# Local attention and FFN block: logits and AV sums by column groups, the AV result turned by DMA, softmax with its maximum, LN2 sums on ScalarE, other FFN groups

## The chip, the cores and the metric

The kernel runs on one core of a Trainium2 chip. The metric is the device time of one launch in microseconds (us). The core has TensorE (PE, matrix products; PEld are its weight loads), VectorE (DVE), ScalarE (ACT), GpSimd (POOL) and SyncE (SP, which here issues nearly all DMAs), all running side by side and waiting for each other by semaphores.

## The reference

A transformer block with adaptive layer norm over 2048 tokens of width 512:

```python
mod = silu(c) @ w_mod                       # shifts, scales, gates: sa, ca, ga, sb, cb, gb
h = layernorm(x) * (1 + ca) + sa            # LN1
q, k, v = h @ wqkv                          # 32 heads of 16
idx = pos[:, None] - 2 * arange(8)          # each token sees itself and 7 earlier ones, 2 apart
logits = einsum('bhsd,bhswd->bhsw', q, k[idx]) * 16 ** -0.5, masked where idx < 0
attn = softmax(logits, axis=-1)             # over the 8 places
o = einsum('bhsw,bhswd->bhsd', attn, v[idx])
x = x + ga * (o @ wo)
h = layernorm(x) * (1 + cb) + sb            # LN2
x = x + gb * ((silu(h @ w1) * (h @ w3)) @ w2)   # FFN of width 1792
```

## The kernel before, in words

Tokens are worked in 16 tiles of 128 (T). Activations are bf16, sums are fp32 in PSUM (8 banks of 128x512). `_build` (L351) records operations with their engine, estimated cost and data; `Program.schedule` (L143) then puts them in an order by a table of priorities (L955) and hands out buffers and banks; `synchronize` (L242) derives the semaphore waits. Each engine then runs its own list strictly in order. The arrays FFN (L341), BLOCKS (L342), DMA_T (L345) and LATE (L347) say which tiles form a group, which groups turn their normalized rows by DMA, and when late weight loads are issued.

The stages, by line:
- The start: warm-up products on ones (L551), modulation columns (L535), gates (L565, spread at L575). SP loads x, the modulation weights and wqkv (all DMAs are issued at L135). LN1 groups of 2, 2, 4, 4, 4 tiles: statistics on DVE (`ln_stats`, L590, L591), the power on POOL (L596, L598), normalizing on DVE (L613), turning on PE (L649), scale and shift on ACT (L657).
- Q and K products (L702), copied by ACT (L710, L711); V products (L721), copied (L731) and stored to DRAM, from where V comes back as shifted rows, 4 loads of 256 KB a tile (in `values`).
- Logits of a tile: DVE multiplies Q with the 8 shifted K (L752, 128x4096); PE sums each head's 16 features: 32 products with the multiplied block (128x128) as weights and a 32-column indicator E moving (L761). Tokens are then on partitions.
- Softmax (`exps`, `softmax`): ACT takes exp straight from PSUM (L775) without a maximum; DVE adds in three steps (L791, L793, L795), takes a reciprocal (L797) and scales (L798); tile 0 is masked by a multiply (L787).
- AV (`values`, L803): the weights go to DRAM and come back turned (two DMAs a tile), DVE multiplies the shifted V by them (L821), PE sums over the 8 places with 32 products of 16 columns (L830), which come out with features on partitions; ACT copies (L836); PE multiplies by wo (L843); DVE adds to x (L847).
- LN2: statistics on DVE as in LN1, the bias on DVE (L603), normalizing on ACT (L609), turning on PE for the first three groups (L649) and by DMA for the last two, modulation on ACT (L657, L634).
- FFN in groups of 2, 4, 4, 4, 2 tiles: 14 slices, each of w1 and w3 products (L859, 256 or 512 columns), silu on ACT (L865), product on DVE (L868); then w2 (L897, halves of 256 columns in the last two tiles, L885), the last add (L907) and the store.

## Time and profile before

| what | before |
|---|---|
| median of 3 runs (lowest to highest) | 250.9 us (250.34 to 252.05) |
| profiled execution: span, first to last instruction | 248.6 us |
| profiled execution: own time | not listed apart from the three runs; their median lies 2.3 us over the span |
| ACT busy | 123.3 us |
| DMA packets, bytes | 49393, 37.09 MB |

The page gives each engine's busy time, then 40 slices of the span, DMA queues, the chain of work that ended last (followed back from the last instruction, at each step to what released it), and groups of equal instructions: line, engine, operation, output and inputs, count, then busy us and mean ns of one, then the idle time of its engine just before them. Products are pipelined, so the mean of one (379 ns for 512 columns) is longer than their spacing. SPq is SP's queue, "issue" time in which nothing shown was waited for.

### The profile page before, as it was taken

Reading aid. Unit: us, or ns where it says so; the run is one execution under the profiler, and the core shown is the slowest. Engines: PE = TensorE matmul, PEld = TensorE weight load, DVE = VectorE, ACT = ScalarE, POOL = GpSimd, SP = SyncE. Lnnn points to the kernel's source line nnn. Section 1 sums busy time; section 2 is a strip of 40 time slices with the busy share of each in tenths; the row PEclk is TensorE's granted clock in tenths of the full one; section 3 lists DMA queues with packets and bytes.
Section 4 is the critical chain, followed back from the end, with each engine's and each line's share of the span. In section 5 each row is a group of like instructions: output and inputs, shape, how many; then the busy total and the mean of one; then the engine's idle time right before and its main releaser. Section 6 shows DMA issues by size and latency. Waiting matters only on the chain.

```text
span 248.6 us, 5772 instructions
## 1 busy us (share of the span) xinstructions
PE 243.5 (98%) x2437; PEld 149.2 (60%) x2437; DVE 186.8 (75%) x289; ACT 123.3 (50%) x216; POOL 21.3 (9%) x48
## 2 busy tenths in 40 slices
PE   8989999999999999999999999999999999999995
PEld 8857665475778856545665564455544444465784
DVE  3869799999898999999899897898942344232442
ACT  2369688864783466943230577443556333110320
POOL 3223500003200110000001101000110000000000
PEclk9999999999999999999999999999999999999999
DMA  6999969679979993336779270436032000001001
GB/s 221 356 327 274 279 201 299 140 199 286 314 223 259 319 288 100 63 54 157 200 232 263 56 229 22 85 46 169 3 84 63 4 0 0 21 24 42 21 3 42
DMA packets 49393, 37.09 MB, mean 149 GB/s; under 512 B 22216, under 2 KB 40664, under 8 KB 49368
## 3 DMA queue, kind: packets, MB, share of 16 engines
q1 hardware_dynamic: 49360, 36.73, 53.3%
q8 instruction: 19, 0.31, 0.5%
q14 instruction: 6, 0.05, 0.1%
q10 hardware_dynamic: 8, 0.00, 0.0%
HBM read 30.67 MB, written 5.26 MB: 145 GB/s over the span
## 4 chain that ended last, share of the span: by engine, by line
PE 94%; DMA 4%; SPq 1%; issue 0%; DVE 0%
PE pall L859 39%; PE pall L897 17%; PE pall L702 11%; PE pall L843 6%; PE pall L721 6%; PE pall L761 5%; PE pall L830 5%; DMA sb_wqkv<-in_A_wqkv_dram 4%; PE pall L885 2%; PE pall L649 2%; SPq L135 1%; PE pall L535 0%; PE pall L565 0%; PE pall L575 0%; DVE sb_o L907 0%
## 5 line engine op out<-in xcount | busy, mean ns | idle before, releaser
L859 PE MATMUL pall<-sb_h,sb_w 128*128 128x512 bf16 (+1 forms) x560 | 101.2, 336 | 0.0
L859 PEld LDWEIGHTS pall<-sb_h,sb_w 128*128 128x128 bf16 x560 | 53.8, 98 | 41.4
L865 ACT ACTIVATE sb_sg<-pall 128x512 bf16<-128x512 f32 (+1 forms) x70 | 35.3, 511 | 64.3 <-PE pall L859 64.3
L868 DVE TENSOR_TENSOR sb_hh<-sb_sg,pall 128x512 bf16<-128x512 bf16 (+1 forms) x70 | 39.0, 575 | 28.4 <-PE pall L859 28.4
L897 PE MATMUL pall<-sb_w,sb_hh 128*128 128x512 bf16 x196 | 44.4, 379 | 0.0
L752 DVE TENSOR_TENSOR sb_pq<-sb_q,sb_kT 128x4096 bf16<-128x4096 bf16 x16 | 36.1, 2280 | 0.5 <-ACT sb_kT L711 0.5
L702 PE MATMUL pall<-sb_h,sb_wqkv 128*128 128x512 bf16 (+1 forms) x160 | 31.0, 336 | 1.4 <-DMA sb_wqkv<-in_A_wqkv_dram 1.4
L897 PEld LDWEIGHTS pall<-sb_w,sb_hh 128*128 128x128 bf16 x196 | 18.9, 98 | 21.1
L821 DVE TENSOR_TENSOR sb_vsh<-sb_vsh,sb_al 128x4096 bf16<-128x4096 bf16 x12 | 27.2, 2283 | 0.4 <-DMA sb_al<-a_scratch_dram 0.2
L590 DVE BATCH_NORM_STATS2 sb_st<-sb_x 128x6 f32<-128x512 bf16 x32 | 21.7, 678 | 4.6 <-DMA sb_x<-in_A_x_dram 4.3
L907 DVE TENSOR_TENSOR sb_o<-pall,sb_x 128x512 bf16<-128x512 f32 (+1 forms) x18 | 11.2, 629 | 17.9 <-PE pall L897 13.6
L657 ACT ACTIVATE sb_h<-pall,sb_modc 128x512 bf16<-128x512 bf16 (+1 forms) x30 | 19.2, 706 | 7.8 <-PE pall L649 7.7
L702 PEld LDWEIGHTS pall<-sb_h,sb_wqkv 128*128 128x128 bf16 x160 | 15.0, 98 | 12.9 <-issue 1.6
L596 POOL TENSOR_TENSOR sb_rs<-sb_mv,sb_cst 128x2 f32<-128x2 f32 x16 | 5.2, 326 | 159.0 <-DVE sb_mv L591 159.0
L609 ACT ACTIVATE sb_xn<-sb_x,sb_nb,sb_rs 128x512 bf16<-128x512 bf16 x16 | 12.1, 805 | 11.5 <-DVE sb_nb L603 11.5
L836 ACT ACTIVATE sb_ot<-pall 128x512 bf16<-128x512 f32 x16 | 9.5, 597 | 15.6 <-PE pall L830 13.7
L761 PEld LDWEIGHTS pall<-sb_E,sb_pq 128*128 128x128 bf16 x512 | 14.8, 96 | 2.9
L843 PE MATMUL pall<-sb_wo,sb_ot 128*128 128x512 bf16 x64 | 15.8, 378 | 0.0
L721 PE MATMUL pall<-sb_wqkv,sb_h 128*128 128x512 bf16 x64 | 15.6, 379 | 0.0
L761 PE MATMUL pall<-sb_E,sb_pq 128*128 128x32 bf16 x512 | 15.0, 176 | 0.0
L598 POOL TENSOR_TENSOR sb_rs<-sb_rs,sb_cst 128x2 f32<-128x2 f32 x16 | 13.9, 871 | 1.3
L710 ACT ACTIVATE sb_q<-pall 128x512 bf16<-128x512 f32 (+1 forms) x20 | 10.2, 517 | 6.6 <-PE pall L702 6.5
(69 smaller groups left out, 196.0 us busy)
## 6 DMA issues: line engine op xcount, KB each, us to landing
sb_vsh<-v_scratch_dram SPq DMA_DIRECT2D x48, 256.0 KB, 4.5
sb_vshx<-v_scratch_dram SPq DMA_DIRECT2D x16, 256.0 KB, 5.3
sb_w<-in_B_w_dram SPq DMA_DIRECT2D x6, 512.0 KB, 7.3
sb_w<-in_B_w_dram SPq DMA_DIRECT2D x6, 384.0 KB, 5.7
v_scratch_dram<-sb_v SPq DMA_DIRECT2D x16, 128.0 KB, 5.3
out_dram<-sb_o SPq DMA_DIRECT2D x14, 128.0 KB, 1.8
sb_wqkv<-in_A_wqkv_dram SPq DMA_DIRECT2D x3, 512.0 KB, 10.0
sb_x<-in_A_x_dram SPq DMA_DIRECT2D x3, 512.0 KB, 10.4
```

The source lines that it names most:

```text
L590: o = p.op("dve", lambda e, m=m, T=T: e.bn_stats(st[:, m, :], x_sb[:, T, :]), 670, ("st", m), r=[vx[T]], w=[vs])
L657: return e.activation(vh.at[:, ft, 0:n * P], b[:, j * 512:j * 512 + n * P], ACT.Identity, bias=modc[:, 8 * which + ft:8 * which + ft + 1], ...
L702: ins = e.matmul(bank(vp)[:, 0:n], wqkv[:, t, col:col + P], vh.at[:, t, 0:n], start=(t == ORDER[0]), stop=(t == ORDER[-1]))
L721: ins = e.matmul(bank(vp), vh.at[:, t, tt * P:(tt + 1) * P], wqkv[:, t, 2 * D:3 * D], start=(t == ORDER[0]), stop=(t == ORDER[-1]))
L752: return e.tensor_tensor(vp.at[:], in0, in1, ALU.mult)
L761: ins = e.matmul(b[:, c0:c0 + H], vp.at[:, w, ft, :], E_sb[:, ft, :], start=(ft == 0), stop=(ft == KT - 1))
L821: return e.tensor_tensor(v_w, v_w, a_w, ALU.mult)
L843: ins = e.matmul(bank(vy), vt.at[:, ft, :], wo[:, ft, :], start=(ft == 0), stop=(ft == KT - 1))
L859: ins = e.matmul(bank(vp)[:, 0:n], wt[:, t, fi * P:(fi + 1) * P], vh.at[:, t, 0:n], start=(t == 0), stop=(t == KT - 1))
L865: p.op("act", lambda e: e.activation(vt.at[:, 0:n], bank(vgp)[:, 0:n], ACT.Silu), c_act(n), k, r=[vgp], w=[vt], table="silu")
L868: p.op("dve", lambda e: e.tensor_tensor(vh_.at[:, 0:n], vt.at[:, 0:n], bank(vup)[:, 0:n], ALU.mult), c_dve(n), k, r=[vt, vup], w=[vh_])
L897: ins = e.matmul(bank(vz), vhh[fi].at[:, tt * P:(tt + 1) * P], w2[:, fi, :], start=(fi == 0), stop=(fi == NF - 1))
```

## The change

- Logits: E becomes the weights, 32 columns wide, and the multiplied block moves, 256 columns at a time; four products write the four groups of 32 PSUM partitions by `tile_position`. 16 products a tile instead of 32; heads now lie on partitions, with 32 tokens and 8 places along the row. Tile 0's mask is a first product that adds a large negative number.
- Softmax: DVE takes the maximum over the 8 places from PSUM and writes the differences; ACT takes exp of them in SBUF; DVE sums in one step, takes the reciprocal and scales. All groups are pairs of tiles.
- The weights are turned by PE (two transposes a tile) and copied by ACT; the DRAM buffer for them is gone.
- AV sums: a 32-column indicator is the weights and the multiplied V moves, 512 columns; 8 products a tile in four column groups. The result has tokens on partitions; ACT copies it and a DMA transpose on SP turns it.
- The residual add also sums its row; LN2 makes its mean from that on POOL, and ACT sums squares of the centred row (`Square` with `accum_out`), 16 of them; POOL makes variance, power and bias. DVE has no LN2 statistics any more.
- FFN groups 2, 2, 4, 4, 2, 2; groups from the third on (12 tiles, formerly 6) are turned by DMA.
- The order of all operations and the buffers are now lists in the file (ORDER, SLOTS), and GATES ties late loads to logits or AV multiplies. In the new order SP issues x rows of tiles 2 to 7, the first gate's weights and x of tiles 8 to 11 ahead of the K weights (before: tiles 2 to 7 alone); the first FFN product stands behind the logits of 9 tiles (before: 8 tiles), and all of LN1, Q, K and V; the third FFN group's first w2 product stands behind all 16 logits. Warm-up products are one of 512 columns in place of four of 128. LN1, Q, K, V, wo and the FFN's arithmetic are as before.

The core of the diff:

```diff
-        p.schedule(_priorities())
+        p.place(ORDER, SLOTS)
-FFN = [[0, 1], [2, 3, 4, 5], [6, 7, 8, 9], [10, 11, 12, 13], [14, 15]]
-BLOCKS = [[[0]], [[1]], [[2, 3]], [[4, 5]], [[6, 7]], [[8, 9]], [[10, 11]], [[12, 13], [14, 15]]]
-VG = 2
+FFN = [[0,1],[2,3],[4,5,6,7],[8,9,10,11],[12,13],[14,15]]
+BLOCKS = [[[0, 1]], [[2, 3]], [[4, 5]], [[6, 7]], [[8, 9]], [[10, 11]], [[12, 13], [14, 15]]]
-DMA_T = (5, 3)
+DMA_T = (5, 2)
+GATES = [-1, 6, 8, 3, 2, 2, 14, 12, 10, 0, 16, 18, 12, 14, 12, 7, 13, 13, 8, 3]
...
+    def ln_sums(Ts):
+
+        n, i, k = len(Ts), Ts[0], ("st", NT + Ts[-1])
+        vnm, vvs, vns = Val("nmean"), [], [Val("xn", xnpool) for T in Ts]
+        p.op("pool", lambda e: e.tensor_scalar(nm[:, i:i + n, 0], sx[:, i:i + n, 0], -1.0 / D, None, op0=ALU.mult), 250, k,
+             r=[vsx[T] for T in Ts], w=[vnm])
+        for T, vn in zip(Ts, vns):
+            vv = Val("var")
+            p.op("act", lambda e, vn=vn, T=T: e.activation(vn.at[:], x_sb[:, T, :], ACT.Square, bias=nm[:, T, :],
+                                                    accum_out=var[:, T, :]), c_act(512) + 230, ("st", NT + T), r=[vx[T], vnm],
+                 w=[vv, vn])
+            vvs.append(vv)
+        va, vr, vb = Val("vare"), Val("rstd"), Val("nbias")
+        rsn = rs[:, NT + i:NT + i + n, 0]
+        o = p.op("pool", lambda e: e.tensor_scalar(rsn, var[:, i:i + n, 0], 1.0 / D, EPS, op0=ALU.mult, op1=ALU.add), 300, k, r=vvs, w=[va])
+        o = p.op("pool", lambda e: e.tensor_tensor(rsn, rsn, bass.AP(cst, 1, [[2, P], [0, n]]), ALU.pow), 600, k, r=[va, vcst],
+                 w=[vr], lead=o)
+        p.op("pool", lambda e: e.tensor_tensor(nb[:, i:i + n, 0], nm[:, i:i + n, 0], rsn, ALU.mult), 250, k, r=[vr, vnm], w=[vb], lead=o)
+        for T, vn in zip(Ts, vns):
+            p.op("act", lambda e, vn=vn, T=T: e.activation(vn.at[:], x_sb[:, T, :], ACT.Identity, bias=nb[:, T, :],
+                                                           scale=rs[:, NT + T, :]),
+                 c_act(512) + 230, ("nm", NT + T), r=[vx[T], vr, vb], w=[vn])
         return vns
 
...
-            def red(e, i=i, vp=vp):
-                b = bank(vl)
-                for w in range(W):
-                    for ft in range(KT):
-                        c0 = i * W * H + w * H
-                        ins = e.matmul(b[:, c0:c0 + H], vp.at[:, w, ft, :], E_sb[:, ft, :], start=(ft == 0),
-                                       stop=(ft == KT - 1))
+            def red(e, i=i, T=T, vp=vp):
+                c0 = vl.at * 512 + i * W * 32
+                if T == 0:
+                    e.matmul(PALL[0:32, c0:c0 + W * 32], ones[:, 0:32], before[:], start=True, stop=False, tile_position=(0, 0))
+                for ft in range(KT):
+                    for q in range(4):
+                        ins = e.matmul(PALL[32 * q:32 * q + 32, c0:c0 + W * 32], E_sb[:, ft, :], bass.AP(vp.at, ft * P + 32 * q, [[W * KT * P, P], [KT * P, W], [1, 2], [2, 16]]),
+                                       start=(ft == 0 and (T > 0 or q > 0)), stop=(ft == KT - 1), tile_position=(0, 32 * q))
                 return ins
 
-            p.op("pe", red, C_RED, ("lg", T), r=[vp, vE], part=[vl])
+            p.op("pe", red, C_RED + (110 if T == 0 else 0), ("lg", T), r=[vp, vE] + ([vbefore, vc] if T == 0 else []), part=[vl], tiled=True)
         return vl
-    def exps(groups, vls):
-
-        ves = [Val("ex", smpool) for _ in groups]
-
-        def ex(e):
-            for Ts, vl, ve in zip(groups, vls, ves):
-                n = len(Ts) * W * H
-                ins = e.activation(ve.at[1].rearrange("p t w h -> p (t w h)")[:, 0:n], bank(vl)[:, 0:n], ACT.Exp)
-            return ins
-
-        p.op("act", ex, sum(c_act(len(g) * W * H) for g in groups), ("ex", groups[0][0]), r=vls, w=ves, table="exp")
-        return ves
-
-    def softmax(Ts, ve):
+    def shift(Ts, vl):
 
         n = len(Ts)
         k = ("sm", Ts[0])
-        o = None
-        if Ts[0] == 0:
-            o = p.op("dve", lambda e: e.tensor_tensor(ve.at[1][:, 0], ve.at[1][:, 0],
-                                                      bass.AP(mask0, 0, [[W, P], [1, W], [0, H]]), ALU.mult),
-                     430, k, r=[vmask0], w=[ve], lock=True)
-        vs1, vs2, vs3, vr, va = Val("s1"), Val("s2"), Val("s3"), Val("rsum"), Val("attn")
-        o = p.op("dve", lambda e: e.tensor_tensor(ve.at[2][:, 0:n], ve.at[1][:, 0:n, 0:4], ve.at[1][:, 0:n, 4:8], ALU.add),
-                 75 + 134 * n, k, r=[ve], w=[vs1], lead=o, lock=True)
-        o = p.op("dve", lambda e: e.tensor_tensor(ve.at[2][:, 0:n, 0:2], ve.at[2][:, 0:n, 0:2], ve.at[2][:, 0:n, 2:4], ALU.add),
-                 75 + 67 * n, k, r=[vs1, ve], w=[vs2], lead=o, lock=True)
-        o = p.op("dve", lambda e: e.tensor_tensor(ve.at[3][:, 0:n], ve.at[2][:, 0:n, 0], ve.at[2][:, 0:n, 1], ALU.add),
-                 75 + 34 * n, k, r=[vs2, ve], w=[vs3], lead=o, lock=True)
-        o = p.op("dve", lambda e: e.reciprocal(ve.at[3][:, 0:n], ve.at[3][:, 0:n]), 75 + 267 * n, k, r=[vs3, ve], w=[vr], lead=o, lock=True)
+        ve, vm, vs = Val("ex", smpool), Val("max"), Val("shifted")
+        o = p.op("dve", lambda e: e.tensor_reduce(ve.at[2][:, 0:n], bass.AP(PALL, bank(vl).offset, [[8 * 512, P], [W * 32, n], [1, 32], [32, W]]),
+                                                  AX.X, ALU.max), 90 + 267 * n, k, r=[vl], w=[vm], hold=[ve], lock=False)
+        p.op("dve", lambda e: e.tensor_tensor(bass.AP(ve.at[1], 0, [[2 * W * 32, P], [W * 32, n], [1, W], [W, 32]]),
+                                              bank(vl)[:, 0:n * W * 32].rearrange("p (n w t) -> p n w t", n=n, w=W),
+                                              bass.AP(ve.at[2], 0, [[64, P], [32, n], [0, W], [1, 32]]), ALU.subtract),
+             100 + 267 * n, k, r=[vl, vm], w=[vs], hold=[ve], lead=o, lock=False)
+        ve.shifted = vs
+        return ve
+
+    def exps(groups, ves):
+
+        vxs = [Val("exp") for _ in groups]
+
+        def ex(e):
+            for Ts, ve in zip(groups, ves):
+                n = len(Ts) * W * 32
+                flat = ve.at[1].rearrange("p n t w -> p (n t w)")[:, 0:n]
+                ins = e.activation(flat, flat, ACT.Exp)
+            return ins
+
+        p.op("act", ex, sum(c_act(len(g) * W * 32) for g in groups), ("ex", groups[0][0]), r=[ve.shifted for ve in ves], w=vxs,
+             hold=ves, table="exp")
+        return vxs
+
+    def softmax(Ts, ve, vx_):
+
+        n = len(Ts)
+        k = ("sm", Ts[0])
+        vs, vr, va = Val("sum"), Val("rsum"), Val("attn")
+        o = p.op("dve", lambda e: e.tensor_reduce(ve.at[3][:, 0:n], ve.at[1][:, 0:n],
+                                                  AX.X, ALU.add), 80 + 267 * n, k, r=[vx_], w=[vs], hold=[ve], lock=True)
+        o = p.op("dve", lambda e: e.reciprocal(ve.at[3][:, 0:n], ve.at[3][:, 0:n]), 75 + 235 * n, k, r=[vs], w=[vr], hold=[ve], lead=o, lock=True)
         p.op("dve", lambda e: e.tensor_tensor(ve.at[0][:, 0:n], ve.at[1][:, 0:n],
-                                              bass.AP(ve.at[3], 0, [[2 * H, P], [H, n], [0, W], [1, H]]), ALU.mult),
-             75 + 267 * n, k, r=[vr, ve], w=[va], lead=o, lock=True)
-        return va
-
-    def values(T, i, ve, va):
-
-
-        vad, val = Val("ad"), Val("al", alpool)
-        p.dma(bass.AP(a_dram, T * P * W * H, [[W * H, 16], [16 * W * H, 8], [1, W * H]]),
-              lambda: ve.at[0][:, i].rearrange("p w h -> p (w h)"), ("ad", T), 65536, r=[va, ve], w=[vad], cost=400)
-        p.dma(lambda: val.at[:], bass.AP(a_dram, T * P * W * H, [[H, P], [16 * W * H, 8], [1, H]]), ("al", T), 65536 * 3,
-              r=[vad], w=[val], cost=400)
+                                              bass.AP(ve.at[3], 0, [[64, P], [32, n], [1, 32], [0, W]]), ALU.mult),
+             100 + 267 * n, k, r=[vr, vx_], w=[va], hold=[ve], lead=o, lock=True)
+        vt, val = Val("ps_at", psum), Val("al", alpool)
+
+        def turn(e):
+            b = bank(vt).bitcast(bf)
+            for i in range(n):
+                at = b[:, i * 256:(i + 1) * 256].rearrange("p (q y h) -> p q y h", q=4, y=2)
+                for y in range(2):
+                    ins = e.transpose(at[:, :, y, :], bass.AP(ve.at[0], i * W * 32 + y * 16 * W, [[2 * W * 32, P], [1, 16 * W]]),
+                                      ident[:])
+            return ins
+
+        p.op("pe", turn, 114 * n, ("at", Ts[0]), r=[va, vident], w=[vt], hold=[ve])
+        p.op("act", lambda e: e.activation(val.at[:, 0:n].rearrange("p n g h -> p (n g h)"), bank(vt).bitcast(bf)[:, 0:2 * n * P], ACT.Copy),
+             c_act(256 * n), ("at", Ts[0]), r=[vt], w=[val])
+        return val
+
+    def values(T, i, val):
+
         vv = Val("vsh", vshpool)
         loads = []
-        for g in range(0, 8, VG):
-            p.dma(lambda g=g: vv.at[:, g:g + VG, :].rearrange("p g d -> p (g d)"),
-                  bass.AP(v_dram, (PAD + T * P + g) * D, [[8 * D, 16], [-DIL * D, W], [1, VG * D]]), ("vl", T), VG * 131072,
-                  r=[vv_dram[T]] + ([vv_dram[T - 1]] if T else [vvpad]), part=[vv], group=loads)
+        for q in range(4):
+            p.dma(lambda q=q: vv.at[:, 2 * q:2 * q + 2, :],
+                  bass.AP(v_dram, (PAD + T * P + 32 * q) * D, [[2 * D, 16], [-DIL * D, W], [1, 2 * D]]), ("vl", T), (128, 2048),
+                  r=[vv_dram[T]] + ([vv_dram[T - 1]] if T else [vvpad]), part=[vv], group=loads, cost=400)
 
         def av(e):
-            a_w = bass.AP(val.at, 0, [[8 * H, P], [H, 8], [0, DH], [1, H]])
+            a_w = bass.AP(val.at, i * 8 * H, [[2 * 8 * H, P], [H, 8], [0, DH], [1, H]])
             v_w = bass.AP(vv.at, 0, [[8 * D, P], [D, 8], [H, DH], [1, H]])
             return e.tensor_tensor(v_w, v_w, a_w, ALU.mult)
 
@@ -824,18 +780,18 @@
         vo = Val("ps_o", psum)
 
         def acc(e):
-            b = bank(vo)
-            for g in range(8):
-                for ft in range(KT):
-                    ins = e.matmul(b[:, ft * P + 16 * g:ft * P + 16 * g + 16], vv.at[:, g, ft * P:(ft + 1) * P], ind[:],
-                                   start=True, stop=True)
+            c0 = vo.at * 512
+            for y in range(2):
+                for q in range(4):
+                    ins = e.matmul(PALL[32 * q:32 * q + 32, c0:c0 + 512], ind[:, y, :], vv.at[:, 2 * q + y, :], start=(y == 0),
+                                   stop=(y == 1), tile_position=(0, 32 * q))
             return ins
 
-        p.op("pe", acc, C_RED, ("ac", T), r=[vv, vind], w=[vo])
+        p.op("pe", acc, C_ACC, ("ac", T), r=[vv, vind], w=[vo], tiled=True)
+        vc_ = Val("ac", acpool)
+        p.op("act", lambda e: e.activation(vc_.at[:], bank(vo), ACT.Copy), c_act(512), ("ac", T), r=[vo], w=[vc_])
         vt = Val("ot", otpool)
-        p.op("act", lambda e: e.activation(vt.at[:].rearrange("p t (s g) -> p t s g", g=8),
-                                           bass.AP(PALL, bank(vo).offset, [[8 * 512, P], [P, KT], [1, 16], [16, 8]]),
-                                           ACT.Copy), c_act(512), ("ac", T), r=[vo], w=[vt])
+        p.dma(lambda: vt.at[:], lambda: vc_.at[:], ("ot", T), (128, 1024), r=[vc_], w=[vt], cost=1250, transpose=True)
         vy = Val("ps_y", psum)
 
         def wop(e):
@@ -844,8 +800,8 @@
             return ins
 
         p.op("pe", wop, 4 * MM, ("wo", T), r=[vt, vsc_wo], w=[vy])
-        p.op("dve", lambda e: e.tensor_tensor(x_sb[:, T, :], bank(vy), x_sb[:, T, :], ALU.add), c_dve(512), ("rs", T), r=[vy],
-             w=[vx[T]])
+        p.op("dve", lambda e: e.scalar_tensor_tensor(x_sb[:, T, :], bank(vy), 1.0, x_sb[:, T, :], op0=ALU.mult, op1=ALU.add,
+                                                     accum_out=sx[:, T, :]), c_dve(512) + 60, ("rs", T), r=[vy], w=[vx[T], vsx[T]])
```

## The prediction

> **What bounds the kernel now.** I read the page's busy times first, then the chain of work that ended last in order of time, then the groups by shape.
>
> ```profile
> PE 243.5 (98%) x2437; PEld 149.2 (60%) x2437; DVE 186.8 (75%) x289; ACT 123.3 (50%) x216; POOL 21.3 (9%) x48
> ...
> PE 94%; DMA 4%; SPq 1%; issue 0%; DVE 0%
> ```
>
> TensorE (PE) is busy for 98% of the span and is 94% of the chain. The chain shows where that begins and ends:
>
> ```profile
> 3.44 9.98 DMA sb_wqkv<-in_A_wqkv_dram
> 13.41 0.14 issue
> 13.55 1.03 PE pall L702 x8
> ...
> 32.26 1.59 PE pall L761 x64
> ...
> 53.48 0.79 PE pall L830 x32
> ...
> 70.83 2.62 PE pall L859 x24
> ...
> 148.51 17.27 PE pall L859 x80
> ...
> 239.91 6.13 PE pall L885 x56
> 246.04 0.02 issue
> ```
>
> The first K product waits for its weights until 13.55; from there to 246.04 (232.5 us) only PE stands in the chain. So time is saved by PE work removed behind 13.55, if nothing becomes late instead. The chain also gives prices: 24 products of 256 columns take 2.62 (0.109 each), 80 of 512 take 17.27 (0.216), one tile's logits (L761) 0.79, its AV sums (L830) 0.785. The next engine is VectorE (DVE); in this row of the table of stretches (PE, weight loads, DVE, ACT, POOL) it is busy 131.1 of 140 us:
>
> ```profile
> 40.00:180.00 140.00, 140.00 (x1579) 82.77 (x1576) 131.12 (x176) 77.86 (x128) 9.07 (x14) 1.00 0.65 172
> ```
>
> So PE's gain is only worth what DVE allows. Groups by shape (the pair behind the bar: busy us, mean ns):
>
> ```profile
> L859 PE MATMUL pall<-sb_h,sb_w 128*128 128x512 bf16 x336 | 74.8, 379 | 0.0
> L859 PEld LDWEIGHTS pall<-sb_h,sb_w 128*128 128x128 bf16 x560 | 53.8, 98 | 41.4
> ...
> L590 DVE BATCH_NORM_STATS2 sb_st<-sb_x 128x6 f32<-128x512 bf16 x32 | 21.7, 678 | 4.6 <-DMA sb_x<-in_A_x_dram 4.3
> ...
> L798 DVE TENSOR_TENSOR sb_attn<-sb_ex,sb_ssum 128x512 bf16<-128x512 f32 x7 | 4.8, 692 | 0.2
> ```
>
> **PE, part by part**, against the 232.5 us.
> - Logits: 32 small products a tile become 16 of 256 columns, four column groups wide. If the four groups run at once a tile costs 4 x 0.109 = 0.44; one after another, 16 x 0.109 = 1.75. I take 0.44: the four write different partitions with different weights, and weight loads lie beside products (53.8 us of loads, no idle before L859's products). 16 x (0.44 - 0.79) = -5.6. Tile 0's mask product: +0.1.
> - AV sums: 8 products of 512 columns, 0.43 to 1.73 a tile, 0.43 taken for the same reason: 16 x (0.43 - 0.785) = -5.7.
> - The weights' turn on PE, in place of the trip through DRAM: 32 transposes at 0.055 (16 take 0.89 in the chain) = +1.8. LN2's 24 transposes that move to DMA: -1.3.
> - Groups 2,2,4,4,2,2: 112 products of 512 columns become 224 of 256: 24.5 - 24.2 = +0.3.
> - Ahead of the first K product the new order puts 19 more Q products (2.1), 8 transposes (0.4), the first gate (0.4) and its spreading (0.2): -3.1 from what follows.
>
> 232.5 - 13.5 = 219.0 us.
> - Its start: SP now issues x rows 2 to 3, x 4 to 7, the gate's weights and x 8 to 11 ahead of the K weights; formerly x 2 to 3 and x 4 to 7 alone. That is 1.05 MB more; the DMAs moved 349 GB/s there, so +3.0 (0 if they share the rings unevenly, 3.3 at the slowest stretch near, 322 GB/s). K starts at 16.55; the work moved ahead fits in the wait.
> - Changes between full-width and column-group products: 21 runs, 42 changes. No row has one. Nearest is what a product lasts beyond the spacing, 379 - 216 = 163 ns, the pipe emptied: 0 to 6.8 us in all. A gain is excluded, as nothing goes. I take half, 3.4: the changed products lie between unlike ones in any case.
>
> PE's last product then ends at 16.55 + 219.0 + 3.4 = 238.95; 2.6 us of last add and store are unchanged: 241.5.
>
> [...] The trace's full-width loads do run beside products.
>
> **DVE.** LN2's sums leave: 16 x (0.678 + 0.181) = -13.7, the bias -1.2. Softmax: 18.7 us of rows become, for each of 8 pairs, four passes over 512 (0.69, as L798) and a reciprocal (0.557): 26.5, so +7.8. The residual add also sums: 0 to 0.15 more each (a 128x2 operation takes 0.154), +1.0 taken. Narrower FFN products: 28 x 0.396 - 14 x 0.667 = +1.7. Net about -4.
>
> Is DVE early enough? The place to look is the first w2 product of the third group; by then PE has done 127.8 us since K's start and 38 of the changes, and 90.7 follow. PE is there at 16.55 + 127.8 + 3.0 = 147.4. DVE's first logits multiply waits for the copy of the last K product of its group: 16.55 + eight products (3.5) + a V product (0.9) + copy and latency 0.6 = 21.55. From it to the FFN product that PE needs there stand 28 multiplies (2.265), 28 passes, 6 reciprocals, 12 residual adds (0.74), 28 and 13 FFN products (0.396, 0.667), 5 scalings (5.6), 8 normalizations, 3 output adds and small ones: 127.4 by rows. All DVE rows add to 195.0 where the engine was busy 186.8 (neighbours overlap), so 122.0. DVE is there at 143.6: 3.8 us of room. The maximum and the subtraction also put DVE between the logits and ACT's exponential; other multiplies stand behind them in DVE's order, so DVE need not idle there, and the room above covers it; once DVE idles for more than 3.8 us, PE waits.
>
> **ACT and POOL.** ACT gains 16 squares (0.8 each), 8 copies of the turn (0.6) and 2.4 from narrower silus: 20 us on 123. In the dense stretch it was busy 78 of 140, so free on average; by order, a group's LN2 ends 13 us of PE work ahead of its first FFN product, against some 6 us of sums, POOL steps (0.3 to 0.9) and normalizing. Cost nothing; if uncovered, 2 us a group. Table loads stay at 8.
>
> **SP and DMA.** 32 issues of the DRAM trip go (0.59 and 0.40: 16 us), and so does its 2.1 + 2.4 us landing. 22 more DMA transposes come, 1.25 us of issue each, 2.4 us to landing. Each AV turn waits for ACT's copy; behind it on SP stand later V loads and stores, ahead of it often four V loads (0.6 each). So the output product comes at the soonest 0.6 + 2.4 + 2.4 = 5.4 us behind the sums. By the new order PE has 5.4 to 21 us of work between them in 15 tiles, and 3.7 us in tile 3. I charge that place 1.7 us (0 to 3.4).
>
> Sum: 241.5 + 1.7 = 243.2 us of span, against 248.6. The median of the runs, 250.9, lies 2.3 over the profiled execution's span; its own time is not listed apart, so I add 2.3: **245.5**.
>
> **Rivals.**
> - *DVE becomes the bound.* It idled 8.9 of 140 us in the dense stretch; 6% of 122 is 7.6, so the place above comes at 151.2, and 151.2 + 90.7 + 0.3 + 2.6 + 1.7 + 2.3 = 248.8. For it: two engines in fixed order now wait for each other. Against: much of that idle was DVE waiting for a later PE. Chance 0.17.
> - *Slower: the turns land late.* If a turn lands only as late as the V loads ahead of it (4.5 us to landing, not 2.4, and its 1.25 behind them), output products come 8.8 us behind the sums. Tiles 1, 3, 5, 7, 9, 11 and 15 then lack 1.7, 5.1, 3.4, 1.8, 1.4, 2.8 and 2.7: 18.9 in place of 1.7, time 262.7. It decides once the lateness sums to over 7 us. Against: transposes landed in 2.4 us among other traffic. Chance 0.09.
> - *The column groups run in turn.* 16 x (1.31 + 1.30) = +41.8, time 287. It needs 0.61 us a group in place of 0.44 to lose everything (5.4 us over 32). Chance 0.05.
> - *The change does all of it for free*: no cost at mode changes and no wait: 240.4. Chance 0.09.
> - The forecast: 0.60, its own range 242 to 248.5.
>
> **The numbers.** About 1% is what a measurement of this kernel tells from no change. Faster takes 0.58 of the forecast, 0.09 of the free case, 0.08 of the DVE case and 0.01 of the late turns: 0.76. Same (248.4 to 253.4): 0.02 + 0.09 + 0.03 = 0.14. Slower: 0.05 + 0.05 = 0.10. The range runs from the free case, 240, to 251, past the DVE case; it leaves out the column groups in turn and most of the late turns.
>
> **What would show it.** Right: 16 logits products in about 0.44 us and 8 AV products in about 0.43 in the chain; K starting near 16.5; DVE's busy time near 183; few PE waits, the longest for the AV turn. Wrong: gaps of 0.1 us or more on both sides of each run of column groups (mode changes); PE waiting for DVE between 60 and 150 us; output products waiting for transposes in many tiles; runs of 1.7 us a tile.

## The result, and the profile after

| | before | after |
|---|---|---|
| median (lowest to highest) | 251.4 us (250.34 to 252.05, 4 runs) | 264.1 us (263.13 to 265.88, 4 runs) |
| profiled execution: span / own time | 248.6 / not listed apart | 264.2 / 265.88 us |

The ratio is 1.051 (95%: 1.046 to 1.056): slower by 5%, where 2% faster was forecast. In the whole document a median takes all runs of a kernel, while a ratio leaves out the slow ones, those over 1.5% above the fastest of the same kernel, so a median can lie above what its ratio says.

The page of the kernel after: busy times, slices of PE, of its granted clock and of the DMA engines (6.6 us each), the main DMA queue's share, and the chain by engine.

```profile
PE 243.4 (92%) x1840; PEld 139.0 (53%) x1840; DVE 186.2 (70%) x276; ACT 141.0 (53%) x273; POOL 27.7 (10%) x66
...
PE   7799989978959898699999996999999999999995
...
PEclk9889999999997999979999999999999999999999
DMA  6982966999999999990349398024401411000001
...
q1 hardware_dynamic: 42384, 37.51, 57.2%
...
PE 67%; DMA 21%; ACT 5%; SPq 2%; issue 2%; DVE 2%
```

PE is busy as long as before (243.4 to 243.5 us), but the span is 15.6 us longer; DMA went from 4% of the chain to 21%. Behind the start, most gaps of PE lie where the DMA row stands at 9. What PE waited for (total us, times, longest):

```profile
PE pall L799 <- DMA sb_ot<-sb_ac: 9.8, 6, 3.0
PE pall L465 <- DMA sb_wm_s<-in_w_mod_dram: 1.9, 1, 1.9
PE pall L480 <- DVE sb_ind L391: 1.5, 1, 1.5
PE pall L799 <- ACT sb_v L671: 1.4, 1, 1.4
PE pall L815 <- DMA sb_w<-in_B_w_dram: 1.2, 1, 1.2
```

L799 is the output product, which waits for the AV result turned by DMA. The chain in order of time shows these places, the new products beside them, and the start:

```profile
1.80 7.65 DMA sb_wm_s<-in_w_mod_dram
...
18.29 2.18 PE pall L642 x20
...
45.64 0.55 PE pall L702 x16
...
48.79 0.55 PE pall L786 x8
...
54.17 6.45 DMA sb_ot<-sb_ac
...
72.84 6.51 DMA sb_ot<-sb_ac
...
81.06 9.72 DMA sb_w<-in_B_w_dram
...
105.22 7.56 DMA sb_ot<-sb_ac
...
134.27 0.99 PE pall L702 x29
```

Sixteen logits products (L702) alone take 0.55, the 32 of two tiles (29 are on record) 0.99; so the four column groups do run at once, as forecast. The K products start at 18.29, not at 16.55. And these turns take 6.5 to 7.6 us where 2.4 was forecast. DMA issues with the median us to landing:

```profile
sb_vsh<-v_scratch_dram SPq DMA_DIRECT2D x44, 256.0 KB, 5.2
...
sb_ot<-sb_ac SPq DMA_TRANSPOSE x16, 5.6
...
sb_h<-sb_xn SPq DMA_TRANSPOSE x12, 2.4
```

The same kind of transpose, 128 KB each, and 5.6 against 2.4 us. The AV turns alone, shortest, median and longest:

```profile
DMA to landing us min/median/max: 2.3/5.6/7.6
```

The last three of them, issued from 193 us on, land in 2.3 us; the first eight, issued between 50 and 112 us, take 5.5 to 7.6. The table of stretches says where each lies (us, PE, weight loads, DVE, ACT, POOL busy, then clock granted, DMA share, GB/s). First after, then before:

```profile
40.00:80.00 40.00, 33.96 (x326) 16.27 (x324) 35.44 (x37) 29.30 (x53) 2.20 (x4) 1.00 0.98 247
80.00:120.00 40.00, 34.94 (x277) 23.10 (x276) 29.75 (x43) 20.52 (x45) 5.15 (x6) 0.92 0.99 224
120.00:160.00 40.00, 38.38 (x283) 20.10 (x282) 36.36 (x44) 23.90 (x43) 5.98 (x11) 1.00 0.57 126
```

```profile
40.00:80.00 40.00, 40.00 (x506) 25.91 (x503) 37.45 (x49) 27.71 (x53) 3.57 (x2) 1.00 0.88 243
80.00:120.00 40.00, 40.00 (x447) 24.05 (x445) 38.73 (x55) 23.38 (x36) 1.77 (x4) 1.00 0.65 161
```

From 40 to 120 us the 16 DMA engines are now taken up for 98 and 99%, before for 88 and 65%, and PE stands idle for 11.1 us of 80. LN2's transposes are issued from 123 us on, where the load is lower.

To compare PE's work by kind I added the time from each product's start to the next one's, idle taken out (the last column is an experiment below):

| PE, us | before | after | no turns, half of V |
|---|---|---|---|
| logits | 12.85 | 8.36 | 8.30 |
| AV sums | 12.85 | 8.23 | 8.17 |
| turn of the weights | 0 | 2.20 | 2.01 |
| transposes of LN1 and LN2 | 5.79 | 5.52 | 5.28 |
| w1, w3 products | 96.93 | 99.66 | 98.32 |
| w2, output, Q, K, V products | 104.22 | 108.62 | 105.36 |
| all, with the rest | 243.5 | 243.4 | 239.1 |
| idle between products | 1.4 | 16.5 | 2.3 |

So PE's work did get shorter, and the 243.4 us of after hide it. The last column's execution had a granted clock of 1.00 throughout and takes 4.3 us less for the same products; after had 0.84 from 9.5 to 12.7 us, 0.61 from there to 15.8, and 0.83 from 80 to 90 and from 110 to 120 us.

### The profile page after: what moved, and what is told of

Same layout as the page of the kernel before. It is cut to its first block, busy times and chain, and to the rows that moved or that the text cites. A ratio compares the mean times of both kernels' runs of the same rounds, so it can differ in the third digit from the quotient of the medians.

```text
span 264.2 us, 4658 instructions
## 1 busy us (share of the span) xinstructions
PE 243.4 (92%) x1840; PEld 139.0 (53%) x1840; DVE 186.2 (70%) x276; ACT 141.0 (53%) x273; POOL 27.7 (10%) x66
## 4 chain that ended last, share of the span: by engine, by line
PE 67%; DMA 21%; ACT 5%; SPq 2%; issue 2%; DVE 2%
PE pall L815 28%; PE pall L853 16%; DMA sb_ot<-sb_ac 12%; PE pall L642 8%; PE pall L799 4%; DMA sb_w<-in_B_w_dram 4%; DMA sb_wm_s<-in_w_mod_dram 3%; ACT sb_h L597 3%; PE pall L786 2%; SPq L124 2%; DMA v_scratch_dram<-sb_v 2%; PE pall L841 2%; PE pall L661 2%; PE pall L702 1%; ACT sb_v L671 1%
## 5 line engine op out<-in xcount | busy, mean ns | idle before, releaser
L815 PE MATMUL pall<-sb_h,sb_w 128*128 128x256 bf16 (+1 forms) x672 | 102.8, 310 | 1.2 <-DMA sb_w<-in_B_w_dram 1.2
L815 PEld LDWEIGHTS pall<-sb_h,sb_w 128*128 128x128 bf16 x672 | 65.4, 99 | 36.8 <-ACT sb_sg L821 1.8
L821 ACT ACTIVATE sb_sg<-pall 128x256 bf16<-128x256 f32 (+1 forms) x84 | 37.7, 453 | 55.8 <-PE pall L815 55.5
L824 DVE TENSOR_TENSOR sb_hh<-sb_sg,pall 128x256 bf16<-128x256 bf16 (+1 forms) x84 | 41.0, 506 | 28.9 <-PE pall L815 25.1
L799 PE MATMUL pall<-sb_wo,sb_ot 128*128 128x512 bf16 x64 | 17.4, 400 | 11.3 <-DMA sb_ot<-sb_ac 9.8
L863 DVE TENSOR_TENSOR sb_o<-pall,sb_x 128x512 bf16<-128x512 f32 (+1 forms) x18 | 11.3, 630 | 18.3 <-PE pall L853 13.9
L597 ACT ACTIVATE sb_h<-pall,sb_modc 128x256 bf16<-128x256 bf16 (+1 forms) x26 | 15.3, 667 | 9.7 <-PE pall L589 9.7
L803 DVE SCALAR_TENSOR_TENSOR sb_x<-pall,sb_x 128x512 bf16<-128x512 f32 x16 | 10.9, 688 | 8.7 <-PE pall L799 8.7
L799 PEld LDWEIGHTS pall<-sb_wo,sb_ot 128*128 128x128 bf16 x64 | 5.9, 100 | 20.6 <-issue 6.5
L543 ACT ACTIVATE sb_xn<-sb_x,sb_nm 128x512 bf16<-128x512 bf16 x16 | 11.4, 715 | 8.2 <-POOL sb_nm L539 8.2
L661 PE MATMUL pall<-sb_wqkv,sb_h 128*128 128x512 bf16 x64 | 15.6, 379 | 0.0
L777 DVE TENSOR_TENSOR sb_vshx<-sb_vshx,sb_al 128x4096 bf16<-128x4096 bf16 x5 | 11.4, 2288 | 5.1 <-DMA sb_vshx<-v_scratch_dram 3.5
L792 ACT ACTIVATE sb_ac<-pall 128x512 bf16<-128x512 f32 x16 | 9.4, 599 | 10.5 <-PE pall L786 10.2
```

The lines of the kernel that those rows point to most:

```text
L543: p.op("act", lambda e, vn=vn, T=T: e.activation(vn.at[:], x_sb[:, T, :], ACT.Square, bias=nm[:, T, :], accum_out=var[:, T, :]), c_act(512 ...
L597: return e.activation(vh.at[:, ft, 0:n * P], b[:, j * 512:j * 512 + n * P], ACT.Identity, bias=modc[:, 8 * which + ft:8 * which + ft + 1], ...
L661: ins = e.matmul(bank(vp), vh.at[:, t, tt * P:(tt + 1) * P], wqkv[:, t, 2 * D:3 * D], start=(t == ORDER[0]), stop=(t == ORDER[-1]))
L777: return e.tensor_tensor(v_w, v_w, a_w, ALU.mult)
L799: ins = e.matmul(bank(vy), vt.at[:, ft, :], wo[:, ft, :], start=(ft == 0), stop=(ft == KT - 1))
L815: ins = e.matmul(bank(vp)[:, 0:n], wt[:, t, fi * P:(fi + 1) * P], vh.at[:, t, 0:n], start=(t == 0), stop=(t == KT - 1))
```

## The experiments

Theory A: the turns by DMA are late, and PE waits for them in its order. It split on the way: A1, they stand behind the loads in SP's queue; A2, they share full DMA engines with the loads, and are themselves part of the load. Rivals: B, the column-group products and their mode changes; C, DVE's longer softmax; S, W, M, O, P and R, each named with its run.

| kernel | median of all runs, us | ratio to before (95%) |
|---|---|---|
| after | 264.1 | 1.051 (1.046 to 1.056) |
| wait for the turn taken away | 262.8 | 1.039 (1.030 to 1.048) |
| all transposes issued by ScalarE | 284.0 | 1.131 (1.125 to 1.137) |
| turn by PE | 259.0 | 1.031 (1.027 to 1.035) |
| AV part as before | 258.2 | 1.028 (1.023 to 1.032) |
| AV part as before, start order | 258.4 | 1.024 (1.016 to 1.031) |
| AV part as before, weights earlier | 259.1 | 1.029 (1.022 to 1.036) |
| AV part as before, without maximum | 257.3 | 1.021 (1.014 to 1.027) |
| AV part as before, all three | 257.1 | 1.022 (1.017 to 1.027) |
| after, half of V | 254.3 | 1.007 (1.003 to 1.011) |
| AV part as before, half of V | 253.3 | 1.006 (1.002 to 1.010) |
| before, half of V | 250.5 | 0.996 (0.993 to 0.999) |
| after, no turns | 254.5 | 1.006 (1.001 to 1.012) |
| after, no turns, half of V | 248.4 | 0.986 (0.981 to 0.992) |
| before, turns added and waited for | 279.1 | 1.106 (1.095 to 1.117) |
| before, turns added | 262.3 | 1.042 (1.039 to 1.046) |
| before, logits part alone | 257.0 | 1.018 (1.010 to 1.026) |

**The wait alone.**

```diff
-                ins = e.matmul(bank(vy), vt.at[:, ft, :], wo[:, ft, :], start=(ft == 0), stop=(ft == KT - 1))
+                ins = e.matmul(bank(vy), wo[:, ft, 0:P], wo[:, ft, :], start=(ft == 0), stop=(ft == KT - 1))
...
-        p.op("pe", wop, 4 * MM, ("wo", T), r=[vt, vsc_wo], w=[vy])
+        p.op("pe", wop, 4 * MM, ("wo", T), r=[vsc_wo], w=[vy])
```

> The changed kernel, with one edit: the four output products of a tile multiply a fixed block (wo itself) instead of the turned AV result, so they wait for no turn. The 16 DMA turns, the AV sums, their copies and all loads stay. Left out: the AV result does not reach the output. Theory A (the turns come late and TensorE waits for them in its order; 11.3 us idle before the output products, and products near them run at a lowered clock): TensorE idle falls from 20.8 to about 9, the clock goes from 0.981 back to 0.99 or more, time 247 to 253 us. Theory B (the new products themselves, mode changes and lowered clock of the column groups): 260 us or more. Theory C (VectorE's longer softmax or ScalarE's sums are behind the delay; the wait moves to the next product that needs them): 257 to 264 us, with new idle before the AV sums or the w2 products.

Measured 262.8 (260.9 by the ratio): theory A in its first form fell. The wait alone is worth 1.4 us by the medians and 3.1 by the ratios, whose intervals together leave some 2.6 us to each side. The wait for turns is gone from PE's list, and others have taken its place:

```profile
PE pall L815 <- DMA sb_w<-in_B_w_dram: 5.6, 1, 5.6
PE pall L465 <- DMA sb_wm_s<-in_w_mod_dram: 2.4, 1, 2.4
PE pall L756 <- DVE sb_attn L746: 1.6, 1, 1.6
```

The first FFN weights now hold PE for 5.6 us in one place. DMA share from 40 to 120 us stays at 0.97 and 0.98. So most of what was lost is not this wait; something behind all of it was late.

**Another queue.** All 28 transposes move to ScalarE's queue, the AV turns right behind their copies, with four buffers for the turned result. The same word goes into LN2's transposes.

```diff
-        p.dma(lambda: vt.at[:], lambda: vc_.at[:], ("ot", T), (128, 1024), r=[vc_], w=[vt], cost=1250, transpose=True)
+        p.dma(lambda: vt.at[:], lambda: vc_.at[:], ("ot", T), (128, 1024), r=[vc_], w=[vt], cost=1250, transpose=True, eng="act")
```

> The changed kernel, with all 28 DMA transposes (16 AV turns, 12 of LN2) issued by ScalarE instead of SyncE, the AV turns right behind their copies; the loads stay on SyncE. Theory A1 (the turns are late because they stand behind V and weight loads in SyncE's queue): landing of an AV turn falls from 5.6 us median to 2.4 to 3.5, the wait before the output products from 11.3 us to under 4, time 250 to 257 us. Theory A2 (they are late because they share the 16 DMA engines with the loads, whatever the queue): landing stays at 5 us or more and the time at 260 to 268 us. Theory B or C: waits at the output products may shrink, the time stays within 2 us of 264. A cost on the way: 28 issues on ScalarE, 1.25 us each at the price seen on SyncE, 35 us on an engine busy for 141.

```profile
sb_vsh<-v_scratch_dram SPq DMA_DIRECT2D x44, 256.0 KB, 6.6
...
sb_ot<-sb_ac ACTq DMA_TRANSPOSE x16, 7.4
```

An AV turn on a queue without loads lands later (7.4 us) and the V loads too (6.6): A1 is out. That the time went to 284.0 no theory foresaw. PE's longest waits are 15.9 us for turns and 5.5 for ACT's normalized rows; how the rest splits I did not settle.

**The turn by PE; the AV part as before.** The first turns the copy by four PE transposes in the sums' own bank, the second takes the 32 old products. Both have four buffers for the turned result in place of two.

```diff
+        def turn(e):
+            b = bank(vo).bitcast(bf)
+            for ft in range(KT):
+                ins = e.transpose(b[:, ft * P:(ft + 1) * P], vc_.at[:, ft * P:(ft + 1) * P], ident[:])
+            return ins
...
-        p.dma(lambda: vt.at[:], lambda: vc_.at[:], ("ot", T), (128, 1024), r=[vc_], w=[vt], cost=1250, transpose=True)
```

```diff
-                    ins = e.matmul(PALL[32 * q:32 * q + 32, c0:c0 + 512], ind[:, y, :], vv.at[:, 2 * q + y, :], start=(y == 0),
-                                   stop=(y == 1), tile_position=(0, 32 * q))
+                    ins = e.matmul(b[:, ft * P + 16 * g:ft * P + 16 * g + 16], vv.at[:, g, ft * P:(ft + 1) * P], ind16[:],
+                                   start=True, stop=True)
```

> The changed kernel, with the AV result turned by TensorE instead of DMA: four transposes a tile from ScalarE's copy into the bank of the sums, 1 to 2.8 us of TensorE work behind the sums, and a second ScalarE copy a tile. Column groups stay. TensorE gets 64 transposes, 0.06 to 0.11 us each (4 to 7 us), ScalarE 16 copies of 0.4 to 0.6 us. Theory A: no wait at the output products, 16 transposes of DMA load gone, 264 - 11.3 - 3 to 5 (clock) + 4 to 7 = 251 to 256 us. Theory B: 267 to 272 us (work added, nothing gained). Theory C: 262 to 268 us.

> The changed kernel, with the AV part alone as in the kernel before: 32 sums a tile with the multiplied V as weights and 16 columns moving, which come out with features on partitions; ScalarE's copy writes the output product's operand; no turn by DMA. Everything else of the change stays. TensorE gets 5.5 us of sums back. Theory A: 264 - 11.3 - 3 to 5 (clock) + 5.5 = 253 to 256 us. Theory B (column groups and their mode changes cost more than they save): 245 to 251 us. Theory C or D (start, loads, softmax): 262 to 270 us.

259.0 and 258.2: 5 to 6 us better, though PE has 4.1 us of transposes (or 5.3 us of longer sums) more. Theory B is out: with and without column groups in AV the time is the same, and the logits, whose column groups stay in both, take 8.36 us in the table above where they took 12.85. Both stay 2 to 3 us over what A said; some of the loss was elsewhere.

**Three places that were left**, on the kernel with the AV part as before: the order of the first loads (S), FFN weights issued ahead of three tiles' V (W), softmax without its maximum (M).

SP's first loads were x 0-1, x 2-3, modulation weights, x 4-7, wq, gate weights, x 12-15, wk, wv; they become x 0-1, modulation weights, x 2-3, wq, x 4-7, gate weights, wk, wv, x 12-15. The second parts of w1 and w3 move in ORDER, with their gates; `shift` with its two DVE passes goes:

```diff
-GATES = [-1, 6, 8, 3, 2, 2, 14, 12, 10, 0, 16, 18, 12, 14, 12, 7, 13, 13, 8, 3]
+GATES = [-1, 6, 8, 3, 2, 2, 14, 12, 10, 0, 14, 14, 12, 14, 12, 7, 13, 13, 8, 3]
...
-                flat = ve.at[1].rearrange("p n t w -> p (n t w)")[:, 0:n]
-                ins = e.activation(flat, flat, ACT.Exp)
+                ins = e.activation(ve.at[1][:, 0:n], bass.AP(PALL, bank(vl).offset, [[8 * 512, P], [W * 32, n], [1, 32], [32, W]]), ACT.Exp)
```

> Base: the changed kernel with the AV part as before (258.2 us), with the first loads in another order: modulation weights right behind x of tiles 0 and 1, x of tiles 12 to 15 behind the V weights. Ahead of the K weights stand 3.5 MB in place of 4.0. Theory S (the start is a part of what is left): modulation starts 0.8 us earlier, the K products 1 to 2 us earlier, time 256 to 257.5. Rival: the time gained is given back at the next wait (V store, weights of the FFN): within 0.6 us of 258.2.

> Base: the changed kernel with the AV part as before (258.2 us), with the second part of w1 and w3 (512 KB each) issued ahead of the V loads of tiles 6, 11 and 7 instead of behind them. In the base TensorE waits 4.1 us for w1 in the first FFN group (issued at 76.8, landed at 86.8 us). Theory W (the FFN was begun early, but its weights stand behind V loads that wait for a buffer): that wait goes, time 253.5 to 255.5. Rival (the DMA engines are full there whatever the order): the V loads land later instead, new waits at the AV sums, 257 to 260.

> Base: the changed kernel with the AV part as before (258.2 us), without the maximum: ScalarE takes exp straight from PSUM, and VectorE's 8 maxima and 8 subtractions (0.68 and 1.09 us each, together 14.2 us) go. Theory M (VectorE's longer softmax holds back the multiplies and so TensorE): 252 to 256 us. Rival (VectorE has the room, as I predicted): 257 to 259 us.

> Base: the changed kernel with the AV part as before (258.2 us), with the start order, the earlier weights and no maximum together. If the three causes add up, the sum of their gains: 248 to 252 us. If one wait stands behind the other, no more than the largest of them, 253 to 256 us.

258.4, 259.1, 257.3 and 257.1: S, W and M fall to their rivals, and all three together missed both answers. None differs from 258.2 by more than the intervals. Taking 14.2 us off DVE moved the time by 1.0 us (1.7 by the ratios, to 256.5, between M's two answers), so theory C is out as the main cause. With the weights earlier, PE no longer waits 4.1 us for w1, but for DVE's multiply of V, whose loads now come later:

```profile
PE pall L787 <- DVE sb_vshx L778: 4.7, 1, 4.7
```

With all three it is 4.4 us at the same place. That is what full DMA engines would look like: the order chose only whether w1 (4.1 us) or V (4.7) was waited for.

**Less load.** Half of each V load left out; instructions, order and waits unchanged.

```diff
-            p.dma(lambda q=q: vv.at[:, 2 * q:2 * q + 2, :],
-                  bass.AP(v_dram, (PAD + T * P + 32 * q) * D, [[2 * D, 16], [-DIL * D, W], [1, 2 * D]]), ("vl", T), (128, 2048),
+            m = 2 if T in (0, 1, 7) else 1
+            p.dma(lambda q=q, m=m: vv.at[:, 2 * q:2 * q + m, :],
+                  bass.AP(v_dram, (PAD + T * P + 32 * q) * D, [[2 * D, 16], [-DIL * D, W], [1, m * D]]), ("vl", T), (128, 2048),
```

> The changed kernel, with half of the shifted V loaded: each of the 4 loads of a tile brings rows of 1024 B in place of 2048 B (tiles 0, 1 and 7 still in full). Left out: every second token's V, for which old data of the buffer is multiplied. Instructions, order and waits stay; only DMA load goes, about 7 MB of 37.8. Theory A2 (the 16 DMA engines are full from 40 to 120 us; turns and weights are late because they share them with V): landing of an AV turn from 5.6 us to 2.5 to 3.5, the wait before the output products from 11.3 to under 4 us, time 249 to 254. Rival R (a turn is slow by itself, or its place in the order decides): landing 5 us or more, time over 260. Rival P (the order and TensorE's work, not DMA): waits shrink but time over 256.

> The same half of V left out, in the changed kernel with the AV part as before (258.2 us, no turn by DMA). Theory A2: what is left over my forecast is DMA too, 249 to 253 us. Rival P (the new order or TensorE's work): 256 us or more.

> Control: the same half of V left out in the kernel before (tiles 0, 1 and 5 in full). It waits for almost nothing (1.4 us on TensorE before the K products), so all theories expect no change: 250 to 251.5 us. If it gets faster by over 1 us, DMA load costs the kernel before too, and the two runs above have to be read against it.

254.3 and 253.3 (each 0.3 over A2's range by the median; 253.1 and 252.8 by the ratios, inside it) and 250.5. In the first the turns land in 3.0 us:

```profile
sb_ot<-sb_ac SPq DMA_TRANSPOSE x16, 3.0
```

and PE's wait for them is a single one:

```profile
PE pall L800 <- DMA sb_ot<-sb_ac: 0.9, 1, 0.9
```

Nothing but bytes was taken away, and 9.8 us went (11.1 by the ratios); the control lost 0.8 (1.1). A2 holds.

**No turns at all**: the output products multiply the unturned copy; the transposes go, then also half of V.

```diff
-        p.dma(lambda: vt.at[:], lambda: vc_.at[:], ("ot", T), (128, 1024), r=[vc_], w=[vt], cost=1250, transpose=True)
...
-                ins = e.matmul(bank(vy), vt.at[:, ft, :], wo[:, ft, :], start=(ft == 0), stop=(ft == KT - 1))
+                ins = e.matmul(bank(vy), vc_.at[:, ft * P:(ft + 1) * P], wo[:, ft, :], start=(ft == 0), stop=(ft == KT - 1))
```

> The changed kernel without any turn of the AV result: the output products multiply ScalarE's copy as it stands (four buffers of it). Left out: the turn, so the output products sum over tokens. Column groups, mode changes and order stay. Theory A2 (16 turns are DMA load in a full stretch): both the wait and the load go, 259.0 less 4.1 us of TensorE's turns, or 258.2 less 4.6 us of the longer sums, 253 to 256 us. Rival (the wait alone, load does not matter): 262 to 264 us, as with the wait alone taken away.

> The changed kernel without the turns (output products on the unturned copy) and with half of V loaded: both loads gone, about 9 MB of 37.8. Left out: the turn and half of V. If the DMA engines are all that was wrong with my sum, what stays is the forecast without its turn charge and with the measured TensorE rows (logits and sums -9.1, turns of weights +2.2, start 0.4 later): 245 to 248 us. If the new order and TensorE's own work miss my sum: 250 to 253 us.

254.5: the turns cost 9.6 us in all (11.3 by the ratios), of which the wait alone was worth 1.4 (3.1); some 8 are left in either count. These need not be the DMA engines' load alone: with the turns go SP's 16 issues of about 1.3 us and the 9.7 us in which SP stood for ACT's copies, with loads queued behind. With half of V SP still stood 9.3 us, and the kernel got faster by as much all the same, so the load is enough to explain it; at full load the two are not separated. And 248.4 with both loads gone, between the two answers (245 to 248, 250 to 253) and 0.4 over the first (247.7 by the ratio, inside it). The stretches of this last kernel, against those of after:

```profile
40.00:80.00 40.00, 39.33 (x378) 21.47 (x377) 38.32 (x43) 31.65 (x63) 5.50 (x7) 1.00 0.79 238
80.00:120.00 40.00, 39.57 (x344) 25.77 (x345) 37.85 (x53) 25.15 (x52) 6.46 (x10) 1.00 0.38 112
```

Same order, same products: PE idle for 1.1 us of 80 in place of 11.1.

**The turns in the old order.** Sixteen transposes added to the kernel before, each on SP behind ACT's copy of the AV result, into a buffer that nothing reads.

```diff
+            o = self.dma(self.tub[n % 2][:], vt.at[:].rearrange("p t c -> p (t c)"), ("ot", T), 131072 * 3, eng="sp", transpose=True)
+            o.deps = {copy: True}
```

> The kernel before in its own order on every engine, with 16 DMA transposes added on SyncE, each right behind ScalarE's copy of the AV result, into a buffer that nothing reads. Theory A2 (the load counts where the DMA engines are full: share 0.76 to 1.08 between 30 and 90 us here too): 252 to 256 us, V and weights landing later. Rival O (the new order, FFN begun early and its weights behind V, is what makes the turns dear): within 1 us of 251.3.

> As the run with turns added to the kernel before, with its flaw mended: there the next user of the output product's bank waited for the added turn, so TensorE stood for turns (11.9 us before FFN products alone) that were meant to be load only. Now only ScalarE's next copy into the same buffer waits, two tiles later. Theory A2 (the load by itself): 252 to 256 us. Rival O (the old order has room for this load): within 1 us of 251.3.

The first (279.1) says nothing on the question, for the flaw told above. The second: 262.3, 11.1 us slower, over both answers. The main queue, before and then here:

```profile
q1 hardware_dynamic: 49360, 36.73, 53.3%
```

```profile
q1 hardware_dynamic: 58064, 38.83, 61.1%
```

Before had 49360 packets at 53.3% of 248.6 us, 132.5 us of all 16 engines; now 61.1% of 261.7 is 159.9. So 16 turns of 128 KB cost 27.4 us, 1.7 each. Only about half is their own: the trace's DMA records have 8192 more packets of 256 B (13.1 us of 16 engines), while the 8704 packets of 2048 B, nearly all V's, rise from 114 to 130 ns each (8.7 us) and the 4 B ones from 10 to 30 ns (4.3 us). Rival O is out: it isn't the new order. One thing isn't separated here: SP stands 13.4 us for ACT's copies with loads queued behind.

**The logits part alone**, without the maximum, in the kernel before, ordered by its own planner.

```diff
-                        ins = e.matmul(b[:, c0:c0 + H], vp.at[:, w, ft, :], E_sb[:, ft, :], start=(ft == 0),
-                                       stop=(ft == KT - 1))
+                        ins = e.matmul(PALL[32 * q:32 * q + 32, c0:c0 + W * 32], E_sb[:, ft, :], bass.AP(vp.at, ft * P + 32 * q, [[W * KT * P, P], [KT * P, W], [1, 2], [2, 16]]),
+                                       start=(ft == 0 and (T > 0 or q > 0)), stop=(ft == KT - 1), tile_position=(0, 32 * q))
```

> The kernel before with the logits part alone: logits by column groups, softmax on heads (without a maximum), attention weights turned by TensorE in place of the two DMAs by DRAM; AV sums, LN2, FFN groups as before; the order made by the planner of the kernel before, with priorities searched anew for these operations. TensorE by the measured rows: logits 12.85 to 8.4 us, turns +2.2, so 2.2 us less work; 32 DMAs fewer. If this part is worth its sum: 248.5 to 250 us. Rival (mode changes and a weaker order eat it): 251 to 254 us.

257.0, slower than either answer. PE's logits fell to 9.1 us, but V landed late and PE stood 3.0 us before the AV sums. It tells of this order, not of the part; whether the part gains in a good order stays open. No version that I tried beat the kernel before without leaving work out.

## Why the prediction was wrong

**The step that failed** is the one under SP and DMA: "22 more DMA transposes come, 1.25 us of issue each, 2.4 us to landing", and from it "the output product comes at the soonest 0.6 + 2.4 + 2.4 = 5.4 us behind the sums", charged 1.7 us in one tile. Two errors are in it. The 2.4 us came from six transposes issued between 156 and 185 us, where the mean DMA share was 0.35; most AV turns had to land where it was 0.88 and 0.65 already and the change raised it to 0.98 and 0.99. They took 5.6 in the median, and 2.3 where the share was 0.15 (193 to 206 us). And a turn was costed as a delay for the product that reads it, not as load for everything else that uses the engines. Measured: 9.6 us for the turns, 1.4 of it by the wait (11.3 and 3.1 by the ratios). The 32 DMAs by DRAM that go I priced by their issues and landing alone; by the trace's DMA records their packets took about 14 us of all 16 engines (16384 of 64 B at 10 ns, 2048 of 512 B at 28 ns), half of what 16 turns cost.

**The bound.** "PE's gain is only worth what DVE allows" looked at engines only. The same row had 0.65 for the DMA engines over 140 us; by parts it was 0.88 and then 0.65, and the change puts more load there.

**Terms of the sum.** Logits and AV sums by column groups: -5.6 and -5.7 forecast, before 3.4 for mode changes; -4.5 and -4.6 measured with most of these in it. The better value of the two bounds was right. A lone run of 16 takes 0.55 where 0.44 is the spacing: 0.11 for two changes, 2.3 us for 21 runs. The turn of the weights: +1.8, measured 2.0 to 2.2. LN2's transposes: -1.3, measured -0.3 to -0.5. FFN of narrower products: +0.3, measured +1.4 without the load and +2.7 with it. The other products cost 4.4 us more than before in the changed kernel and 1.1 without the load; around PE's waits its granted clock was lower too (0.92 from 80 to 120 us).

K's start: 16.55 forecast for the K weights' sake, 18.29 measured, and not by these weights. The modulation weights landed at 9.45, and from there PE worked through the order ahead of K without a gap to fit the moved work in. Without turns and with half of V the same work ended at 16.92, 0.4 over the forecast; the other 1.4 us go with the granted clock, 0.61 in after from 12.7 to 15.8 us and 1.00 there: 13 of the products in between took 2.23 and 1.42 us. (The x rows issued ahead of the K weights are those of tiles 12 to 15, not 8 to 11 as told above; the bytes are the same.)

Without turns and with half of V the kernel takes 248.4, against 245.5 less the 1.7 charged for the turn: the rest of the sum is short by 4.6 us (4.1 in span, 245.6 against 241.5). The table gives 2.6 of it (239.1 - 243.5 = -4.4, forecast -7.0), K's start 0.4; the rest has no row of its own. (PE's work before and behind the w2 product, 127.8 and 90.7, adds to 218.5 where the sum has 219.0; the DVE rival would be 249.3.)

**DVE and ACT** were as forecast: 186 and 141 us of busy time (183 and 143 forecast), the subtraction dearer (1.09 for 0.69), and DVE is 2% of the chain; without the maximum the time moved by 1.0 us.

**The rivals.** "The turns land late" gave 262.7, near the result, with a chance of 0.09; its lateness was real, its mechanism only half of it, since the wait alone was worth 1.4 us (3.1 by the ratios) and not 17. That its number came so near is luck. What I held against it, "transposes landed in 2.4 us among other traffic", did not hold: there was little other traffic. DVE as the bound, the groups in turn, and the free case are out.

**Mode changes, column groups and transposes.** For each mode change I had put 0.081 us, half of the 0.163 that a product lasts beyond the spacing. A lone run of 16 logits products took 0.55 us where 0.44 is the spacing; put down to its two changes that is about 0.055 each, a third of the 0.163. All four column groups ran at once, their weight loads (94 ns each) beside them: 16 more products add 0.44 us, 0.99 against 0.55. The turns by DMA cost more than other traffic: in the kernel before with 16 added, their own packets took 0.8 us of all engines for 128 KB, and 1.7 with what they did to the others, where before's whole load, 36.73 MB in 132.5 us, comes to 0.47 us for as much.

## What to carry to other kernels

A DMA put in place of engine work is load before it is latency: here 16 turns cost 9.6 us, 1.4 of it by the wait (11.3 and 3.1 by the ratios). So before taking one as free, read the DMA share in the very stretch where it will run (0.88 and 0.65 before, 0.98 and 0.99 after), and cost it in time of all engines, its effect on the other packets included (1.7 us for a turn, 0.8 of it its own). Take a landing time only for the load at which it was seen (here 2.3 us at a share of 0.15, 5.5 to 7.6 at 0.98 and 0.99). Where taking a wait away moves the time little and the waits change their names, look for a shared resource, and test it by taking bytes away at unchanged order (here half of V, 9.8 us).

## What the hardware showed that I had not expected

- A transposing DMA of 128 KB came as 512 packets of 256 B (23.6 ns each on average in the changed kernel), and in the kernel before with 16 of them added, packets of 2048 B took 130 ns on average in place of 114 (150 in the changed kernel with all transposes on ScalarE's queue, 132 with them on SP's).
- In one and the same kernel an AV turn landed in 2.3 us where the DMA share was 0.15 (the last three, 193 to 206 us) and in 5.5 to 7.6 where it was 0.98 and 0.99 (the first eight, 40 to 120 us).
- Issuing all transposes from another engine's queue made the AV turns land later, 7.4 in place of 5.6 us.
- Around PE's waits of up to 3 us the granted clock was 0.83 in the stretches 80 to 90 and 110 to 120 us of the changed kernel; the kernel before had 1.00 there. Behind the wait of 1.9 us at the start it was 0.61 from 12.7 to 15.8 us.
- The subtraction, a DVE pass over 512 fp32 elements written with a stride, takes 1.09 us, where other passes over 512 take 0.68 to 0.69. Whether the stride is the reason was not shown: no run changes it alone.
